# Query loads of the second half merged from four to two per pair, and the first two w_in tiles issued between the pairs

## The chip, the cores and the metric

One core of one Trainium2 chip. The metric is device time in microseconds (us) of one execution, taken as the median of several runs.

## What is computed

Attention with a bias that depends on the distance of two positions, followed by a two-layer MLP whose activation is the square of relu. Batch 4, 8 heads, 576 positions, head size 64; the MLP takes 2304 tokens of 512 to 2048 and back.

```python
scores = scale * np.matmul(q, k.transpose(0, 1, 3, 2))          # q, k, v: (4, 8, 576, 64)
x = (log1p(abs(i - j)) / log1p(max(i, 1)))[..., None]
bias = np.maximum(x @ w1 + b1, 0.0) @ w2                        # per head
attn = softmax(scores + bias, axis=-1)
y = np.matmul(attn, v)                                          # tokens of 512
out = np.maximum(y @ w_in, 0.0) ** 2 @ w_out                    # w_in (512, 2048), w_out (2048, 512)
```

## The kernel before

**Units and halves.** The heads are taken in pairs: `(b, hp)` is batch b and head pair hp. A unit `(b, hp, ic)` is one block of 128 query rows of one pair, both heads (ic 0 to 3), or the last 64 rows of both (ic 4, `TAIL`). There are 80 units (`units`, L125 to L127). The first 40 are batches 0 and 1 (`AB` = 2), ordered so that each block of bias is shared by all eight pairs. The second 40 (from `NA` = 40) are batches 2 and 3, ordered pair by pair: units 40 to 44 are the first pair, 45 to 49 the second.

**A unit.** `scores(u)` (L410) multiplies q and k on PE into the PSUM tile `sp` (one buffer), DVE adds the bias and finds the row maximum (L434, two instructions in a full unit; called the reduction below), ACT takes the exponential (L439). Two units later come `transposes` (PE L484, L487 and ACT copies L485, L488), then `values` (PE L502, and the DVE copy L507). After the last unit of a pair `normalise` and `scale_x` follow (PE L456, L470; DVE L473).

**Loads.** All loads are issued from the SP queue in one order. `load_k` makes two loads, `load_q` (L146) four: for each head one of 64 x 64 (the tail rows, L150) and one of 64 x 512 (L151) into a tile of 576 columns. In memory the queries lie as five blocks of 128 columns per head; in the last block the first head has its 64 rows in columns 0 to 63 and the second head in columns 64 to 127, and the rest is zero. In the second half k and q lie in tiles of which there are three, in space that the tiles of the first half leave.

**The loop** over s (L628) traces the program: at s = 40 it opens the pools of the second half and issues k and q of the first three pairs (L637 to L639); a further pair follows at s = 45, and so on; v loads come at L641.

**Weights.** w_in has 16 tiles of 512 KB. Before they can be used, their common scale must be known, so each is loaded once only for its largest element: `load_w` into a `stage` tile (two buffers) and `scan_w` (a DVE reduction, L189 reading `stage`). At s = 40 (`SC` - 1), after k and q of the three pairs, the first two are issued (L642 to L644). From s = 41 on, ten units hold the 16 scans, and each scan is followed by the load of the tile after next (L654) into the buffer that it frees. They are called w0 to w15 below, in the order of the scans. From s = 53 on the first 12 tiles are loaded again and split into two parts (`split_in`), between the units. The MLP follows.

**What sets the order.** A planner lays out the instructions of each queue (PE, DVE, ACT, POOL, SP) in advance from simulated times, and the hardware takes each queue in that order. `keep_in_program_order` pins an instruction behind what was traced before it on its engine: the scan of w0 thus can't be planned ahead of the reduction of unit 41, those of w1 and w2 not ahead of that of unit 42, and that of w3 not ahead of that of unit 43. What a scan waits for, everything behind it on DVE waits for too.

Of the kernel before, what the change touches and what calls it, by code (L numbers as in the profile page):

```python
# [10 lines left out]
F32 = mybir.dt.float32  # L11
# [10 lines left out]
B, H, S, D = 4, 8, 576, 64  # L22
# [5 lines left out]
AB = 2  # L28
NF = DFF // 128
NIC = 5  # L30
TAIL = 4
# [4 lines left out]
WB, WS, LW, XS, XB, LAG, NE, SC, SN, AH = 40, 3, 4, 48, 70, 1, 13, 22, 16, 2  # L36
# [13 lines left out]
SC = 41  # L50
# [29 lines left out]
def attention_then_relu2_mlp(ctx: ExitStack, tc: tile.TileContext, q, k, v, cols, w_in, w_out, psi, xmat, dist, out):  # L80
    nc = tc.nc
    PE, DVE, ACT, POOL, SP = nc.tensor, nc.vector, nc.scalar, nc.gpsimd, nc.sync
# [61 lines left out]
        v_t[b, hp] = t  # L144

    def load_q(b, hp):  # L146
        t = kq_p[-1].tile([128, S], F32, name="q1", tag="q1")
        for h in range(2):
            rows = slice(64 * h, 64 * h + 64)
            SP.dma_start(out=t[rows, 512:], in_=q[b, hp, TAIL, :, h, rows])  # L150
            SP.dma_start(out=t[rows, :512].rearrange("d (i m) -> d i m", i=TAIL), in_=q[b, hp, :TAIL, :, h].rearrange("i d m -> d i m"))  # L151
        q_t[b, hp] = t

    stage_p = {}
    w_t, wraw_t = {}, {}  # L160
# [249 lines left out]
    def scores(u):  # L410
        b, hp, ic = units[u]
        kt, qt = k1_t[b, hp], q_t[b, hp]
        negm = att.tile([128, 2], F32, name="negm", tag="negm", bufs=3)
        if (b, hp) not in sum_t:
            sum_t[b, hp] = att.tile([128, 9], F32, name="sums", tag="sums", bufs=AB * HP + 2)
        sums = sum_t[b, hp]
        p = att.tile([128, 2 * S], F32, name="p", tag="p", bufs=PB)

        nsp = 2 if ic < TAIL else 1
        sp4 = ps.tile([128, 4, 512], F32, name="sp", tag="sp", bufs=1)  # L420
        sps = [sp4[:, 2 * n:2 * n + 2] for n in range(nsp)]
        cols = slice(128 * ic, 128 * ic + 128 if ic < TAIL else S)

        for m, (x, h) in enumerate((x, h) for x in range(2) for h in (1, 0)):
            rows = slice(64 * h, 64 * h + 64)
            k0 = HALF * x + (64 if h and ic == TAIL else 0)
            out_t, to = (sps[h], slice(0, 128)) if ic < TAIL else (sps[0], rows)
            mm = PE.matmul(out_t[to, x, :HALF], lhsT=qt[rows, cols], rhs=kt[rows, k0:k0 + HALF], start=True, stop=True)  # L428
            if m:
                tc.keep_in_program_order(mm)  # L430
        for n, sp in enumerate(sps):
            bias = bias_t[:, 9 * hp + 2 * ic + n]
            t = att.tile([128, S], F32, name="t", tag="t", bufs=TB)
            DVE.tensor_tensor_reduce(  # L434
                out=t.rearrange("p (x n) -> p x n", x=2), in0=sp[:, :, :HALF],
                in1=bias.rearrange("p (x n) -> p x n", x=2), scale=-0.125, scalar=3.0e38,
                op0=ALU.add, op1=ALU.min, accum_out=negm[:, n:n + 1],
            )
            ACT.activation(out=p[:, S * n:S * n + S], in_=t, func=AF.Exp, bias=negm[:, n:n + 1], scale=-1.0, accum_out=sums[:, 2 * ic + n:2 * ic + n + 1])  # L439
        p_t[u] = p  # L440
        if ic == TAIL:
            POOL.tensor_copy(out=p[:, S:S + 64], in_=p[:, S - 64:S])
# [185 lines left out]
    for s in range(NU + TL + 1):  # L628
# [7 lines left out]
        for m, g in enumerate(groups[AB * HP:]):  # L636
            if s == max(first[g] - KL, NA):  # L637
                load_k(*g)
                load_q(*g)  # L639
            if s == max(first[g] - KL + TL + 1, NA - AB * HP + 2 + TL + m):  # L640
                load_v(*g)  # L641
        if s == SC - 1:  # L642
            load_w(ins[0])
            load_w(ins[1])  # L644
        for n in early:
            if when[n] == s + LW:
                load_w(n)
# [242 lines left out]
```

## Time and profile before

| | |
|---|---|
| median of 3 runs | 798.25 us (797.27 to 798.29) |
| profiled execution, its own time | 797.97 us |
| its span | 796.2 us |
| PE busy | 723.5 us, 91% of the span |
| DVE busy | 574.5 us, 72% |
| ACT busy | 456.5 us, 57% |
| DMA | 50.14 MB |

Times inside the execution are us from the start of the span. PE is TensorE's matmul, DVE VectorE, ACT ScalarE, POOL GpSimd; SPq is SP's queue, which issues loads. In a row of a timeline the number in square brackets is the time the engine was idle just before, with what ended it. The rows that matter stand in the section after the next.

### The profile page before, as it was taken

The numbers are of one execution on the slowest core, as the hardware profiler recorded it, in microseconds if no ns is written. First come the engines' busy times: TensorE is split into PE (matmuls) and PEld (weight loads), VectorE is DVE, ScalarE is ACT, GpSimd is POOL, SyncE is SP. The second block draws the span as 40 slices with busy tenths as digits, with TensorE's granted clock in tenths as the row PEclk, the third lists the DMA queues.
The fourth block names the chain that finished last, engine by engine and source line by source line (L and its number), as shares of the span: only waits on it lengthen the run. The fifth ranks groups of instructions, "written<-read, shape, count | busy, mean of one in ns | idle before, by whom it ended". The sixth has DMA issues, their size and how long they took to land.

```text
span 796.2 us, 17616 instructions
## 1 busy us (share of the span) xinstructions
PE 723.5 (91%) x7094; PEld 571.7 (72%) x7094; DVE 574.5 (72%) x1215; ACT 456.5 (57%) x940; POOL 186.4 (23%) x295
## 2 busy tenths in 40 slices
PE   5499999999988999979889899999989999999992
PEld 5456778787756676656677677878768887888881
DVE  7867778785666678898897979784845576557661
ACT  5757777777655678888676656664442233224220
POOL 1444333232210023342223324250400021000000
PEclk7869999999989999999999999999999999999997
DMA  7610000000376522301231143001010001000100
GB/s 203 191 60 18 3 16 2 3 2 2 105 239 232 189 85 85 111 28 54 80 107 54 67 146 107 28 22 59 26 54 1 1 1 54 1 1 1 54 2 27
DMA packets 27990, 50.14 MB, mean 63 GB/s; under 512 B 5252, under 2 KB 13444, under 8 KB 27908
## 3 DMA queue, kind: packets, MB, share of 16 engines
q1 hardware_dynamic: 27908, 49.01, 18.8%
q8 instruction: 56, 0.92, 0.5%
q14 instruction: 26, 0.21, 0.1%
HBM read 43.23 MB, written 5.77 MB: 62 GB/s over the span
## 4 chain that ended last, share of the span: by engine, by line
PE 50%; DVE 19%; ACT 8%; DMA 7%; SPq 6%; issue 5%; POOL 3%; DVEq 0%; ACTq 0%; POOLq 0%
PE y L766 16%; PE ha L717 8%; PE sp L428 7%; PE px L502 6%; PE hb L717 5%; PE pp L484 4%; PE bb L383 4%; DMA stage<-in_w_in 3%; DVE t L434 3%; ACT p L439 2%; SPq L150 2%; SPq L151 2%; DVE area L618 2%; DVE gl L747 1%; DVE wa L185 1%
## 5 line engine op out<-in xcount | busy, mean ns | idle before, releaser
L766 PE MATMUL y<-w,gh 128*128 128x512 f32 x576 | 177.9, 401 | 2.5 <-ACT gh L746 1.3
L717 PEld LDWEIGHTS <-area 128*128 128x128 f16 x1680 | 147.4, 99 | 42.5 <-issue 15.3
L439 ACT ACTIVATE p<-t,negm 128x576 f32<-128x576 f32 x144 | 111.2, 775 | 27.0 <-DVE negm L434 26.8
L434 DVE CUSTOM_DVE_ANT_0 t<-sp,area 128x576 f32<-128x576 f32 x144 | 104.1, 752 | 30.0 <-PE sp L428 21.3
L766 PEld LDWEIGHTS y<-w,gh 128*128 128x128 f32 x576 | 105.9, 190 | 24.9 <-ACT gh L746 2.9
L428 PE MATMUL sp<-k,q 64*128 64x288 f32 (+1 forms) x640 | 108.2, 447 | 15.0 <-DVE negm L434 11.4
L717 PE MATMUL ha<-area 128*128 128x256 f16 (+1 forms) x960 | 106.3, 266 | 9.0 <-DVE area L734 4.9
L766 PE MATMUL y<-w,gl 128*128 128x512 f32 x288 | 107.5, 397 | 1.1 <-DVE gl L747 1.1
L502 PE MATMUL px<-pt,v 128*64 128x128 f32 (+1 forms) x1600 | 96.6, 267 | 3.5 <-DVE xT L507 2.0
L485 ACT COPY pt<-pp 128x512 f32<-128x512 f32 x144 | 79.7, 582 | 32.0 <-PE pp L484 31.9
L502 PEld LDWEIGHTS px<-pt,v 128*64 128x64 f32 x1600 | 79.2, 137 | 19.7 <-issue 8.2
L484 PE MATMUL pp<-ident,p 128*128 128x128 f32 x576 | 84.5, 283 | 5.5 <-ACT pt L485 2.4
L428 PEld LDWEIGHTS sp<-k,q 64*128 64x128 f32 (+1 forms) x640 | 55.9, 182 | 41.1 <-DVE negm L434 15.3
L717 PE MATMUL hb<-area 128*128 128x256 f16 (+1 forms) x720 | 79.9, 262 | 1.4 <-DVE area L618 0.9
L484 PEld LDWEIGHTS pp<-ident,p 128*128 128x128 f32 x576 | 62.0, 142 | 22.8 <-issue 7.4
L398 POOL TENSOR_TENSOR area<-bt,bt 128x256 f32<-128x256 f32 x72 | 53.2, 763 | 81.9 <-DVE bt L393 81.9
L383 PE MATMUL bb<-wmov,mask 128*128 128x64 f16 x1440 | 52.6, 199 | 14.3 <-DVE bt L404 11.0
L766 PEld LDWEIGHTS y<-w,gl 128*128 128x128 f32 x288 | 53.8, 189 | 13.6 <-DVE gl L747 2.2
L383 PEld LDWEIGHTS <-mask 128*128 128x128 f16 x1440 | 48.2, 102 | 21.3 <-DVE bt L404 11.8
L369 DVE TENSOR_TENSOR mask<-sdist,theta 128x1024 f16<-128x1024 f16 (+1 forms) x78 | 49.7, 669 | 9.4 <-PE bb L383 9.4
L615 POOL TENSOR_TENSOR area<-xT 128x512 f32<-128x512 f32 (+1 forms) x17 | 22.8, 1344 | 143.2 <-DVE area L618 143.2
L747 DVE TENSOR_TENSOR gl<-area,gh 128x512 fp32r<-128x512 f32 (+1 forms) x40 | 30.2, 776 | 24.1 <-ACT gh L746 17.2
(153 smaller groups left out, 945.9 us busy)
## 6 DMA issues: line engine op xcount, KB each, us to landing
stage<-in_w_in SPq DMA_DIRECT2D x32, 512.0 KB, 4.2
stage<-in_w_out SPq DMA_DIRECT2D x16, 512.0 KB, 3.5
v<-in_v SPq DMA_DIRECT2D x16, 320.0 KB, 3.8
out<-o SPq DMA_DIRECT2D x18, 256.0 KB, 2.0
q<-in_q SPq DMA_DIRECT2D x32, 128.0 KB, 3.3
k<-in_k SPq DMA_DIRECT2D x16, 160.0 KB, 3.7
k<-in_k SPq DMA_DIRECT2D x16, 144.0 KB, 3.7
xc<-in_xmat SPq DMA_DIRECT2D x5, 288.0 KB, 3.6
```

The source lines that it names most:

```text
L369: DVE.tensor_tensor(out=m[:, :, :w], in0=win, in1=th.to_broadcast([128, 8, w]), op=ALU.is_ge)
L383: PE.matmul(bb[:, 64 * (7 - r):64 * (8 - r)], lhsT=m[:, r], rhs=wmov[:, n], start=(n == 0), stop=(n == 1))
L398: POOL.tensor_tensor(out=dst, in0=tw, in1=sw, op=ALU.add)
L428: mm = PE.matmul(out_t[to, x, :HALF], lhsT=qt[rows, cols], rhs=kt[rows, k0:k0 + HALF], start=True, stop=True)
L434: DVE.tensor_tensor_reduce(out=t.rearrange("p (x n) -> p x n", x=2), in0=sp[:, :, :HALF], in1=bias.rearrange("p (x n) -> p x n", x=2), sca ...
L439: ACT.activation(out=p[:, S * n:S * n + S], in_=t, func=AF.Exp, bias=negm[:, n:n + 1], scale=-1.0, accum_out=sums[:, 2 * ic + n:2 * ic + n ...
L484: PE.transpose(pp[:, 128 * c:128 * c + 128], p[:, k0:k0 + 128], ident)
L485: ACT.copy(pt[:, 4 * h:4 * h + 4], pp.rearrange("p (c m) -> p c m", c=4))
L502: PE.matmul(px[64 * h:64 * h + 64, :w], lhsT=vt[:, c, h], rhs=src, start=(c == 0), stop=(c == 4))
L717: PE.matmul(h[:, s, :w], lhsT=a, rhs=x, start=(k == 0), stop=(k == 5))
L747: DVE.tensor_tensor(out=gl, in0=g, in1=gh.bitcast(F32), op=ALU.subtract)
L766: PE.matmul(y, lhsT=a[:, slot, o:o + 128], rhs=x, start=((n, P) in firsts and f == 0 and m == 0), stop=((n, P) in lasts and f == 1 and m = ...
```

## The change

For batches 2 and 3 `load_q` makes one load per head: all five blocks of 128 columns go into a tile of 640 columns as they lie in memory, the zero columns too. The tail unit of the second head therefore reads its queries at column 576 instead of 512 (`q0`); all matmuls keep their shapes. And w0 is issued after k and q of the first pair and w1 after those of the second, instead of both after the third. The first half keeps its loads.

```diff
     def load_q(b, hp):
+        if b >= AB:
+            t = kq_p[-1].tile([128, NIC * 128], F32, name="q1", tag="q1")
+            for h in range(2):
+                SP.dma_start(out=t[64 * h:64 * h + 64].rearrange("d (i m) -> d i m", i=NIC), in_=q[b, hp, :, :, h].rearrange("i d m -> d i m"))
+            q_t[b, hp] = t
+            return
         t = kq_p[-1].tile([128, S], F32, name="q1", tag="q1")
...
-        cols = slice(128 * ic, 128 * ic + 128 if ic < TAIL else S)
...
+            q0 = 128 * ic + (64 if h and ic == TAIL and b >= AB else 0)
+            cols = slice(q0, q0 + (128 if ic < TAIL else 64))
...
                 load_k(*g)
                 load_q(*g)
+                if s == SC - 1 and m < 2:
+                    load_w(ins[m])
...
-        if s == SC - 1:
-            load_w(ins[0])
-            load_w(ins[1])
```

## Rows read from the trace of the kernel before

**Rows 1.** Timeline of DVE: start, duration, line, operation [idle before, releaser]

```profile
222.20 0.75 DVE L434 CUSTOM_DVE_ANT_0 t<-sp,area 128x576 f32<-128x576 f32 x1
...
223.93 0.22 DVE L473 TENSOR_TENSOR xT<-xT,rt 128x64 f32<-128x64 f32 x1
227.74 0.69 DVE L189 TENSOR_REDUCE small<-stage 128x1 f32<-128x512 f32 x1 [3.60 <-DMA stage<-in_w_in]
...
228.94 0.75 DVE L434 CUSTOM_DVE_ANT_0 t<-sp,area 128x576 f32<-128x576 f32 x1
...
230.29 0.68 DVE L189 TENSOR_REDUCE small<-stage 128x1 f32<-128x512 f32 x1
```

**Rows 2.** Timeline of PE, same columns

```profile
216.34 1.24 PE L428 MATMUL sp<-k,q 64*128 64x288 f32 x6
...
223.24 1.24 PE L428 MATMUL sp<-k,q 64*128 64x288 f32 x8
...
226.78 0.23 PE L456 MATMUL rp<-ident_b,parts 128*27 128x128 bf16 x1
230.43 2.29 PE L428 MATMUL sp<-k,q 64*128 64x288 f32 x8 [3.42 <-DVE negm L434]
```

**Rows 3.** Timeline of SP's queue: start, time to the group's end, line, load

```profile
210.02 0.47 SPq L137 DMA_DIRECT2D k<-in_k  x1
...
211.18 0.60 SPq L150 DMA_DIRECT2D q<-in_q  x1
...
213.56 0.62 SPq L151 DMA_DIRECT2D q<-in_q  x1
...
223.51 1.02 SPq L172 DMA_DIRECT2D stage<-in_w_in  x2
224.63 1.54 SPq L143 DMA_DIRECT2D v<-in_v  x3
228.46 2.87 SPq L172 DMA_DIRECT2D stage<-in_w_in  x2
```

**Rows 4.** Instructions of the tile stage, 200 to 300: ns min/median/max, first to last start

```profile
L189 DVE TENSOR_REDUCE small<-stage x16: 681/686/689, 227.7 to 270.0; 128x1 f32<-128x512 f32 x16
...
DMA to landing us min/median/max: 3.4/4.3/5.6
```

**Rows 5.** Stretches: busy of PE, PEld, DVE, ACT, POOL, PEclk, DMA share, GB/s

```profile
228.00:230.00 2.00, 0.00 (x0) 0.00 (x0) 2.00 (x5) 0.27 (x1) 0.00 (x0) 0.91 1.01 387
230.00:232.00 2.00, 1.57 (x6) 1.19 (x8) 1.17 (x4) 1.50 (x5) 0.00 (x0) 0.50 0.95 352
...
234.00:236.00 2.00, 2.00 (x9) 1.31 (x9) 1.88 (x6) 1.31 (x4) 0.00 (x0) 0.50 0.86 268
```

**Rows 6.** Chain that ended last, 223 to 270: start, us, what

```profile
231.00 5.57 DMA stage<-in_w_in
...
263.88 1.73 SPq L150
...
265.71 4.22 DMA stage<-in_w_in
```

**Rows 7.** Timeline of PE, later

```profile
250.84 1.31 PE L502 MATMUL px<-pt,v 128*64 128x128 f32 x20 [1.96 <-DVE xT L507]
...
271.57 0.35 PE L198 MATMUL pw<-small,ones 128*128 128x1 f32 x2 [0.72 <-DVE small L218]
```

**Rows 8.** Page, DMA issues: count, KB each, median us from issue to landing

```profile
k<-in_k SPq DMA_DIRECT2D x16, 160.0 KB, 3.7
...
q<-in_q SPq DMA_DIRECT2D x32, 16.0 KB, 2.9
```

**Rows 9.** Instructions of line 398, the last writers of the first half's bias

```profile
L398 POOL TENSOR_TENSOR area<-bt,bt x72: 721/737/1188, 46.6 to 181.1; 128x256 f32<-128x256 f32 x72
```

**Rows 10.** Stretches of the weight splits, columns as in Rows 5

```profile
300.00:350.00 50.00, 44.09 (x478) 31.94 (x472) 44.93 (x103) 42.18 (x97) 18.61 (x32) 1.00 0.24 78
350.00:400.00 50.00, 43.47 (x478) 32.78 (x474) 40.88 (x100) 37.60 (x84) 15.63 (x34) 0.97 0.21 72
```

## The prediction

> **What bounds the kernel now.** Over the whole span PE is the busiest engine, but an average says nothing about the one place that the change touches, so I read that place: the handover from the first half to the second, some 20 us after 210. I began with the DVE timeline, because the scans of w_in stand in it between the reductions that PE waits for. After the scaling of a finished pair had ended at 223.93 + 0.22 = 224.15, DVE sat idle for 3.60 us until w0 had landed at 227.74 [rows 1]. Behind that scan stands the reduction of unit 42, at 228.94. Its scores had been on PE at 223.24 for 1.24 us, so they were ready at 224.5: the reduction was some 4.4 us late, and only for the scan [rows 1, 2]. The scores of unit 43 need the PSUM buffer that this reduction empties. So PE ran dry at 226.78 + 0.23 = 227.0 and stood 3.42 us [rows 2]. That is one stall, seen on two engines; it counts once.
>
> Why w0 came late is in SP's queue. Its first load of the second half goes out at 210.02, and then k and q of three pairs, 6 loads each, fill the queue until w0 goes at 223.51. It lands 4.2 us later [rows 1, 3]. The 16 scans run from 227.7 to 270.0, one buffer being refilled while the other is scanned [rows 4]; the chain that ended last runs through such a refill at 231.00 (5.57 us) and one at 265.71 (4.22 us) [rows 6]. PE waits for this chain again at 250.84 (1.96 us, for a DVE copy queued behind a scan) and at 271.57 (0.72 us) [rows 7]. From 223 to 270, then, the time is set by scans and refills rather than by PE's work; what starts the scans earlier moves the whole stretch.
>
> **The change part by part.**
>
> *The queries.* A q load costs SP about the same whether small or large: the first is issued at 211.18, the fourth at 213.56, so (213.56 - 211.18) / 3 = 0.79 us apart, and one alone takes 0.60 or 0.62 [rows 3]. Two fewer save 1.2 to 1.6 us of SP per pair, 1.4 for the sum. The Trainium skill (DMA: Bandwidth & Descriptors, Rules for kernel authors) says that many small transfers should be made one, since under 64 KB one mostly pays overhead; the 16 KB load here took 2.9 us to land and the 160 KB one 3.7, so the trace bears that out, but it gives the sum nothing that SP's rows don't. A merged load of 160 KB should land like the k load of 160 KB, in 3.7 us [rows 8]. For the first pair the second q load goes out at about 212.0 and lands at 215.7; before, the fourth went at 213.56. PE reached the scores of unit 40 at 216.34 without having been idle [rows 2], so the earlier landing is worth nothing, and the 0.6 us between 215.7 and 216.34 is its cover. If the load lands like the slowest here, in 5.57 us [rows 6], PE waits 212.0 + 5.57 - 216.34 = 1.2 us. I take 0, ends 0 and a loss of 1.2. The 32 KB of zeros per head are in the same transfers and cost nothing of their own. The matmuls keep their shapes: nothing. The wider tile shifts where the three buffers lie in the space of the first half's tiles; these are all free when the last scores of that half are done, which is when the first k load went, so the loads can go no later for it: nothing.
>
> *w0 and w1.* In the new order w0 stands behind 4 loads instead of 18: 210.02 + two k loads at some 0.6 + two q loads at 0.6 to 0.8 gives 212.6 instead of 223.51, and w1 about 3.1 us later, at 215.7. Its wait: a stage buffer lies in space of the first half's preparation, whose last write ended soon after 181.1 [rows 9], long before. Even with the longest landing, 5.6 us [rows 4], w0 is there at 218.2 and w1 at 221.3. The scan of w0 can't be planned ahead of unit 41's second reduction, which follows that at 222.20 [rows 1]; so it finds its data, and starts when DVE comes to it, at 224.15: 227.74 - 224.15 = 3.6 us earlier. Unit 42's reduction follows at about 225.4, after its scores (224.5), so these don't hold it. The scan of w1 moves from 230.29 to 226.7 and finds its data too. w2 and w3 are issued when these two scans free the buffers, so they move by the same 3.6, and so on down the chain. k and q of the second and third pair now stand behind one or two weight tiles, 0.5 us of SP each, and share the DMA engines with them; they are needed five and ten units later, so this is hidden by some 15 us.
>
> *The refills beside the v loads.* Before, three v loads went out right behind w1 [rows 3], and at 228 to 230 the DMA engines were full (share 1.01, 387 GB/s) [rows 5]; w3's refill took 5.57 us against a median of 4.3 [rows 4, 6]. With SP empty some 4 us earlier these v loads mostly land before w2 and w3 are issued, so up to 5.57 - 4.3 = 1.3 us more. I take 0.7, ends 0 and 1.3.
>
> *The later q loads.* They stand on SP between refills. At 263.88 one took 1.73 us directly ahead of the refill that landed at 269.93 [rows 6], and behind that scan PE waited 0.72 us [rows 7]. With two q loads fewer that refill goes up to 2.3 us earlier, but PE can win only what it waited. I take 0.7, ends 0 and 1.5 (there are waits behind it too).
>
> *The clock.* After PE had been empty from 228 to 230 the granted clock was 0.50 from 230 to 236, the level of 1.2 GHz; PE was busy 1.57 + 2.00 + 2.00 = 5.6 us of it (three rows, the first and last shown) [rows 5]. At full clock that work would take 2.8 us less. But in that stretch PE runs beside the chain of scans, which waits for refills, so I take 0 for it; ends 0 and 2.8.
>
> *The rest.* Nothing after 270 is tied to a fixed time: the splits and the MLP start when what they read is there. I let the shift go through to the end.
>
> Sum: 3.6 + 0.7 + 0.7 = 5.0 us. Against the profiled execution, 797.97 us in all with a span of 796.2, that gives 793.0; the median of the runs is 0.28 above that execution, so the forecast of the median is **793.2**.
>
> **The rivals.**
>
> *The refill is held instead (A).* SP takes its loads in one order, and the w2 refill at 228.46 stands behind the v loads [rows 3]. A v load needs the buffer of a pair whose values are still being worked on; the last values of unit 39 end at about 226.8 on PE [rows 2]. If the planner puts that v load ahead of w2, w2 goes at 227.3 instead of 224.9. Then 228.46 - 227.3 = 1.2 us is left of the 3.6, and with half of the other terms (0.7) 798.25 - 1.9 = 796.4. The Trainium skill (DMA: Bandwidth & Descriptors, Anatomy of one DMA) says that a semaphore wait is taken by the issuing sequencer before a DMA goes out, which is how such a v load would hold what stands behind it; the order in the rows agrees. For this rival: three v loads follow right behind w1. Against it: SP had issued those three by 224.63 + 1.54 = 226.2, before the values of unit 39 ended.
>
> *Slower by the new plan (B).* All queues from unit 40 on are laid out anew. The tight place is the split of the first tiles, 300 to 400: DVE is busy 44.9 and 40.9 of 50 us, ACT 42.2 and 37.6, and PE stands 100 - 44.1 - 43.5 = 12.4 us [rows 10], since pieces of a split stand in DVE's and ACT's order ahead of a reduction or an exponential. If the new plan puts more of them ahead, PE's idle time grows. It decides from 5.0 + 1.6 = 6.6 us more, half as much again as now; at 8 us more the time is 798.25 + 3 = 801.3. For it: small gaps there depend on the order. Against it: the pieces and their pins are the same.
>
> *The clock counts in full (C).* If PE's slow work was on the path after all, 5.0 + 2.8 = 7.8 us: 790.4.
>
> *It doesn't do what it says (D).* If the planner leaves w0 behind the third pair, or its buffer comes free as late as that, only 2 x 3 loads' worth of SP is saved in front of it, 3 x 1.4 = 4.2 us. That would still cover the 3.6; only if SP is held elsewhere does 0.7 remain: 797.5.
>
> **How the numbers follow.** Forecast (790.8 to 795.5): 0.55. A: 0.20, B: 0.13, C: 0.08, D: 0.04. A measurement of this kernel can tell 0.2%, 1.6 us, so faster means under 796.65 and slower over 799.85. Faster is the forecast, C and 0.08 of A, whose price lies on the border: 0.71. Slower is B: 0.13. Between: 0.16. The range goes from 790.0, which leaves out half of C, to 798.6, which takes in A and D and leaves out B.
>
> **What would show it.** The first stage load on SP at about 212.6, with the k of the second pair behind it. The first scan on DVE at about 223 to 224 without a wait, and no stall of PE at 227; the granted clock at 1.00 from 228 to 238. The second and third refill (w2, w3) issued near 225 and 227.5, landing in about 4.3 us. The last scan near 265 instead of 270.0. If the first scan starts early and the last ends at 269 all the same, the chain is bound by its refills in a way I have not seen (A). If the last scan is 5 us early and the end is not, look at PE's idle time from 300 to 400 (B). A wait of PE for q at 216 would show that the w tiles slow the first pair's queries.

## The result, and the profile after

The changed kernel is slower: 801.42 us median (800.61 to 802.18, 4 runs) against 797.83 (797.27 to 798.29, 4 runs) of the kernel before, a ratio of 1.0057 with a 95% interval of 1.0038 to 1.0077. That is little, and it rests on four runs each; two more kernels with the same new order, run later beside the kernel before, were slower than it too (e2 and e3 below). The profiled execution took 802.18 us with a span of 800.4 (before: 797.97 and 796.2). Line numbers behind the new `load_q` are shifted: scores L430, reduction L436, exponential L441, scans L190, transposes L486 and L489, values L504, copies L509, weight loads L173; L150 is the merged q load.

The issues moved as forecast. This is SP's queue after, against [rows 3]:

```profile
209.53 1.69 SPq L150 DMA_DIRECT2D q<-in_q  x2
211.33 0.54 SPq L173 DMA_DIRECT2D stage<-in_w_in  x1
...
214.46 0.61 SPq L173 DMA_DIRECT2D stage<-in_w_in  x1
...
220.99 0.33 SPq L173 DMA_DIRECT2D stage<-in_w_in  x1
223.23 0.33 SPq L143 DMA_DIRECT2D v<-in_v  x1
```

w0 goes out 2.96 us after the first k load (208.37), where 13.5 us lay between them before. On DVE, against [rows 1], the scans of w0 and w1 find their data, and the stall has moved to w2:

```profile
220.28 0.68 DVE L190 TENSOR_REDUCE small<-stage 128x1 f32<-128x512 f32 x1
...
223.94 0.68 DVE L190 TENSOR_REDUCE small<-stage 128x1 f32<-128x512 f32 x1
227.80 0.69 DVE L190 TENSOR_REDUCE small<-stage 128x1 f32<-128x512 f32 x1 [3.18 <-DMA stage<-in_w_in]
228.40 0.28 DVE L509 COPY xT<-px 128x128 f32<-128x128 f32 x1
```

Two things are to be seen. The first scan starts 7.5 us earlier than before (220.28 against 227.74; 1.65 of it because this execution was that much ahead already at unit 39), more than was forecast. And the last line: a copy out of PSUM, of values that PE had started at 221.88 and finished 1.31 us later, at 223.2, stands behind three scans in DVE's order. PE pays for it, and also for a wait on q that wasn't there before; timeline of PE after, against [rows 2]:

```profile
213.72 1.33 PE L430 MATMUL sp<-k,q 64*128 64x288 f32 x8 [1.38 <-DMA q<-in_q]
...
225.34 0.66 PE L486 MATMUL pp<-ident,p 128*128 128x128 f32 x4
228.74 0.66 PE L486 MATMUL pp<-ident,p 128*128 128x128 f32 x4 [2.73 <-DVE xT L509]
```

The stretches after, columns as in [rows 5], show PE empty at 226 to 228 and the clock at the 1.2 GHz level behind it, and the DMA engines nearly full from 212 on:

```profile
212.00:214.00 2.00, 0.62 (x12) 0.52 (x14) 1.80 (x6) 0.33 (x3) 0.98 (x5) 1.00 0.92 264
...
220.00:222.00 2.00, 1.71 (x13) 0.95 (x13) 2.00 (x6) 2.00 (x6) 0.36 (x1) 1.00 1.15 224
...
226.00:228.00 2.00, 0.00 (x1) 0.00 (x0) 0.20 (x1) 0.58 (x1) 0.00 (x0) 1.00 0.84 329
...
230.00:232.00 2.00, 2.00 (x21) 1.56 (x17) 0.12 (x2) 1.70 (x6) 0.00 (x0) 0.50 0.52 209
```

The tile stage after, against [rows 4], and the chain that ended last, against [rows 6]. The scans start 7.5 us earlier and the last starts where it did before (269.9 against 270.0), and two refills of that chain took 6.78 and 7.35 us, where the longest landing before was 5.6 [rows 4]:

```profile
L190 DVE TENSOR_REDUCE small<-stage x16: 674/686/700, 220.3 to 269.9; 128x1 f32<-128x512 f32 x16
...
DMA to landing us min/median/max: 3.3/4.7/7.5
```

```profile
220.99 6.78 DMA stage<-in_w_in
...
240.07 7.35 DMA stage<-in_w_in
...
264.92 4.99 DMA stage<-in_w_in
```

At the end of this stretch PE waits three times and then runs slow. Timeline of PE after, against [rows 7], and two stretches of it:

```profile
266.67 1.24 PE L430 MATMUL sp<-k,q 64*128 64x288 f32 x8 [1.41 <-DVE negm L436]
269.05 1.31 PE L504 MATMUL px<-pt,v 128*64 128x128 f32 x20 [1.15 <-DVE xT L509]
272.57 1.24 PE L430 MATMUL sp<-k,q 64*128 64x288 f32 x8 [2.20 <-DVE small L218]
...
275.07 2.40 PE L504 MATMUL px<-pt,v 128*64 128x128 f32 x20
```

```profile
270.00:272.00 2.00, 0.37 (x8) 0.12 (x4) 1.93 (x6) 0.22 (x1) 0.00 (x0) 1.00 0.89 295
...
274.00:276.00 2.00, 2.00 (x17) 1.67 (x18) 1.84 (x8) 0.98 (x3) 0.00 (x0) 0.54 0.02 8
```

The values at 275.07 took 2.40 us for what takes 1.31 at full clock. Before, the row sum `pw` and the transposes stood ahead of the scores of unit 52 there, and PE waited 0.72 us [rows 7]. After, they stand behind them, and PE waits 2.20.

To see where the time went I took, for each unit, the end of its last reduction on DVE, counted from that of unit 39, and subtracted the same of the kernel before. Negative is ahead of the kernel before. The column heads are the experiments below.

| unit (before, us) | after | e1 | e2 | e4 | e6 | e10 | e11 | e12 |
|---|---|---|---|---|---|---|---|---|
| 42 (230.3) | -4.70 | -3.73 | +0.27 | -3.99 | -3.73 | -3.73 | -3.73 | -3.73 |
| 43 (235.1) | +0.77 | -4.00 | +3.80 | -0.04 | -3.73 | -4.96 | -2.25 | -3.56 |
| 45 (244.9) | +1.27 | -4.51 | +3.82 | +0.47 | -4.24 | -6.18 | -2.91 | -2.65 |
| 47 (255.4) | +0.55 | -4.02 | +2.05 | -1.15 | +0.21 | -3.88 | +1.52 | -3.61 |
| 50 (266.9) | +1.17 | -4.17 | +1.13 | -1.21 | -0.47 | -4.04 | +1.11 | -2.85 |
| 52 (275.7) | +1.25 | -3.09 | +3.13 | -0.42 | +0.85 | -3.25 | +3.69 | -1.70 |
| 53 (279.3) | +4.54 | -3.09 | +5.98 | -0.42 | +4.66 | -3.26 | +4.89 | +0.75 |
| 54 (281.6) | +4.55 | -3.09 | +5.99 | -0.42 | +4.68 | -3.25 | +4.89 | +0.77 |
| 78 (383.7) | +4.55 | -2.79 | +6.07 | -0.37 | +4.72 | -3.04 | +4.31 | +1.04 |

After unit 53 the lag of the changed kernel stays as it is up to unit 78: the splits of 300 to 400 [rows 10] and all of attention behind them add nothing. The 5 us or so were lost between 210 and 280. The MLP behind it added 1.3 us to the lag in this one execution; in those of the columns e1, e6 and e10 it took 2.4, 2.0 and 3.9 us off, so what a single execution does there says little.

### The profile page after: what moved, and what is told of

It reads as the page before. It is cut to its first block, busy times and chain, and to the rows that moved or that the text cites. A ratio compares the mean times of both kernels' runs of the same rounds, so it can differ in the third digit from the quotient of the medians.

```text
span 800.4 us, 17593 instructions
## 1 busy us (share of the span) xinstructions
PE 720.8 (90%) x7094; PEld 569.8 (71%) x7094; DVE 576.9 (72%) x1215; ACT 455.7 (57%) x940; POOL 188.5 (24%) x295
## 4 chain that ended last, share of the span: by engine, by line
PE 52%; DVE 22%; ACT 8%; DMA 7%; issue 5%; POOL 3%; SPq 0%; DVEq 0%; ACTq 0%; POOLq 0%
PE y L767 16%; PE sp L430 7%; PE ha L718 7%; PE px L504 6%; PE hb L718 5%; PE pp L486 5%; PE bb L384 4%; DMA stage<-in_w_in 3%; DVE t L436 3%; DVE gl L748 2%; ACT p L441 2%; DVE area L620 2%; DMA stage<-in_w_out 1%; DVE wa L186 1%; DVE area L229 1%
## 5 line engine op out<-in xcount | busy, mean ns | idle before, releaser
L441 ACT ACTIVATE p<-t,negm 128x576 f32<-128x576 f32 x144 | 111.2, 776 | 26.2 <-DVE negm L436 26.1
L436 DVE CUSTOM_DVE_ANT_0 t<-sp,area 128x576 f32<-128x576 f32 x144 | 103.9, 751 | 29.6 <-PE sp L430 26.2
L430 PE MATMUL sp<-k,q 64*128 64x288 f32 (+1 forms) x640 | 106.2, 440 | 17.2 <-DVE negm L436 10.7
L504 PE MATMUL px<-pt,v 128*64 128x128 f32 (+1 forms) x1600 | 98.7, 271 | 4.3 <-DVE xT L509 2.6
L504 PEld LDWEIGHTS px<-pt,v 128*64 128x64 f32 x1600 | 80.9, 139 | 20.9 <-issue 7.2
L486 PE MATMUL pp<-ident,p 128*128 128x128 f32 x576 | 84.0, 282 | 7.4 <-DVE xT L509 2.7
L430 PEld LDWEIGHTS sp<-k,q 64*128 64x128 f32 (+1 forms) x640 | 55.4, 179 | 41.9 <-issue 13.9
L486 PEld LDWEIGHTS pp<-ident,p 128*128 128x128 f32 x576 | 61.8, 142 | 25.0 <-issue 7.2
L384 PE MATMUL bb<-wmov,mask 128*128 128x64 f16 x1440 | 50.9, 196 | 14.3 <-DVE bt L405 11.0
L748 DVE TENSOR_TENSOR gl<-area,gh 128x512 fp32r<-128x512 f32 (+1 forms) x40 | 32.4, 831 | 24.5 <-ACT gh L747 17.7
```

What stands on the lines that cost most here:

```text
L384: PE.matmul(bb[:, 64 * (7 - r):64 * (8 - r)], lhsT=m[:, r], rhs=wmov[:, n], start=(n == 0), stop=(n == 1))
L436: DVE.tensor_tensor_reduce(out=t.rearrange("p (x n) -> p x n", x=2), in0=sp[:, :, :HALF], in1=bias.rearrange("p (x n) -> p x n", x=2), sca ...
L486: PE.transpose(pp[:, 128 * c:128 * c + 128], p[:, k0:k0 + 128], ident)
L504: PE.matmul(px[64 * h:64 * h + 64, :w], lhsT=vt[:, c, h], rhs=src, start=(c == 0), stop=(c == 4))
L748: DVE.tensor_tensor(out=gl, in0=g, in1=gh.bitcast(F32), op=ALU.subtract)
```

## The experiments

Two explanations stood against each other from here. **Theory O**: the planner laid out PE's, DVE's and ACT's queues anew, and it is this new order that costs. The instructions are the same; from unit 40 on they stand in another order, and before that in the same one. **Theory L**: the loads collide. SP now issues w0, w1 and the merged q loads so closely that the DMA engines are nearly full from 212 on (share 0.92 to 1.15), refills land late, and everything behind a scan is held.

To part order from loads I made kernels that carry the planned order of another kernel along: each instruction of PE, DVE and ACT between two marks is tied to the one ahead of it in a recorded list. No semaphore wait is added by that; only the planner is bound, and POOL's queue, which the expectation of e1 names too, is left to it. "Old order" is the order of the kernel before, "new order" that of the changed kernel. All ratios are to runs of the kernel before, made beside each kernel; single executions of one kernel with ten or more runs spread over 4 to 9 us there, and so a lag in the table, which is that of one execution, counts only where the ratio agrees.

| | loads | order | median us (runs) | ratio | 95% interval |
|---|---|---|---|---|---|
| after | new | new | 801.42 (4) | 1.0057 | 1.0038 to 1.0077 |
| e1 | new | old | 795.23 (12) | 0.9982 | 0.9966 to 0.9998 |
| e2 | old | new | 804.60 (4) | 1.0099 | 1.0082 to 1.0116 |
| e3 | q merged alone | its own, the new one | 803.59 (6) | 1.0092 | 1.0072 to 1.0112 |
| e4 | w0, w1 moved alone | its own, nearly the old one | 798.22 (12) | 1.0015 | 0.9991 to 1.0039 |
| e5 | new | new to unit 46, then old | 794.57 (10) | 0.9986 | 0.9965 to 1.0006 |
| e6 | new | old to unit 46, then new | 801.85 (4) | 1.0073 | 1.0046 to 1.0099 |
| e7 | new, q rows contiguous | old | 795.38 (12) | 0.9984 | 0.9963 to 1.0006 |
| e8 | new | its own, scans tied behind copies | 799.31 (12) | 1.0043 | 1.0022 to 1.0065 |
| e9 | new | new, old at unit 52 | 800.78 (12) | 1.0043 | 1.0020 to 1.0065 |
| e10 | q of a pair in one load | old | 793.99 (12) | 0.9965 | 0.9940 to 0.9990 |
| e11 | new | old, new for units 47 to 50 | 798.63 (12) | 1.0014 | 0.9987 to 1.0041 |
| e12 | new | old, new from unit 52 on | 798.85 (12) | 1.0033 | 1.0008 to 1.0057 |

### e1: the new loads in the old order

```diff
+def queues_as_recorded(tc):
...
+    traced = {}
+    for i in tc.nc.cur_bb.bb.instructions:
+        traced.setdefault(str(i.engine), []).append(i)
+    dep = mybir.DependencyInfo(mybir.DependencyClass.NoSync, mybir.DependencyReason.DATA)
+    for e, order in json.loads(zlib.decompress(base64.b85decode(RECORDED))).items():
+        for x, y in zip(order, order[1:]):
+            tc.add_manual_dep(traced[e][y], traced[e][x].name, dep, reason="recorded order")
...
         attention_then_relu2_mlp(tc, **args)
+        queues_as_recorded(tc)
```

`RECORDED`, left out here, holds the order of the kernel before.

> The loads of the changed kernel, but PE, DVE, ACT and POOL take their instructions in the order of the kernel before. Theory L (early w tiles and merged q loads fill the DMA engines from 212 to 226, so that the refill of w2 and the first q land late, and that is the loss): still slow, 800 to 802 us. Theory O (the planner's new order costs the time, the loads themselves gain): 793 to 796 us. Both half: 797 to 799.

Measured: 0.9982, faster than the kernel before by 1.4 us (0.2 to 2.7), and 6 us faster than the changed kernel, whose loads are the same. DVE's timeline of this kernel:

```profile
223.86 0.68 DVE L190 TENSOR_REDUCE small<-stage 128x1 f32<-128x512 f32 x1
...
226.40 0.68 DVE L190 TENSOR_REDUCE small<-stage 128x1 f32<-128x512 f32 x1
227.00 0.28 DVE L509 COPY xT<-px 128x128 f32<-128x128 f32 x1
228.94 0.69 DVE L190 TENSOR_REDUCE small<-stage 128x1 f32<-128x512 f32 x1 [1.67 <-DMA stage<-in_w_in]
```

w0 and w1 are scanned without a wait at 223.86 and 226.40 (the forecast said 224.15 and 226.7), and the copy stands ahead of the scan of w2, not behind it. Unit 42 is 3.73 us ahead. The DMA engines are just as full as in the changed kernel, 1.02 over 212 to 226 at 272 GB/s against 1.05 at 274, and here it costs a wait of 1.67 us on DVE. Theory L alone can't be the loss.

### e2: the old loads in the new order

The same edit on the kernel before, with the order of the changed kernel recorded.

> The loads of the kernel before (four q loads, w0 and w1 behind the third pair), but the compute queues in the order of the changed kernel. Theory O: the order alone costs the loss and w0 comes late as well, 801 to 805 us. Theory L: the order costs nothing, 797 to 799 us.

Measured: 1.0099, that is 7.9 us slower (6.5 to 9.2) with not one load changed. Timeline of PE of this kernel:

```profile
216.10 1.31 PE L428 MATMUL sp<-k,q 64*128 64x288 f32 x8 [2.31 <-DMA q<-in_q]
...
228.02 0.41 PE L470 MATMUL ra<-rows,pick 27*64 27x128 bf16 x8 [2.32 <-DVE xT L473]
...
230.58 2.29 PE L428 MATMUL sp<-k,q 64*128 64x288 f32 x8 [2.10 <-DVE negm L434]
```

The new order asks for q earlier, and PE stands 2.31 us for it, with transposes and values of earlier units behind the scores that it could have done; the second and third row show two more waits, for DVE. With e1 this is a square of four kernels: the loads are worth -1.4 us in the old order and 4.5 - 7.9 = -3.4 in the new one (each within 1.3 and 2.1), and the order costs +7.9 with the old loads and some +6 with the new. Order is the loss, and the loads are a gain in both, a small one in the old.

### e3 and e4: which half of the change brings the new order

e3 has the merged q loads alone (the diff without its last two parts), e4 the moved weight loads alone (only those).

```diff
                 load_k(*g)
                 load_q(*g)
+                if s == SC - 1 and m < 2:
+                    load_w(ins[m])
...
-        if s == SC - 1:
-            load_w(ins[0])
-            load_w(ins[1])
```

This is e4, with the q loads of before.

> Only the q loads are merged; w0 and w1 stay behind the third pair. The planner lays out the same compute order as for the whole change. Theory O: slow like the old loads in the new order, 800 to 804 us. Theory L: the w tiles are no longer in the way of q, so about 797 to 799 us.

> Only w0 and w1 are moved between the pairs; q comes in four loads. The planner keeps the order of the kernel before but for a few DVE instructions. Theory O: the stall at the first scan goes and nothing else changes, 793 to 796 us. Theory L: the w tiles fill the DMA engines ahead of the v loads and w2, so 798 to 802 us.

e3 gave 1.0092, and its planned order of PE, DVE and ACT is that of the changed kernel, instruction for instruction. So merging the q loads is what turns the order over. PE's order in the traces is the same in both, too. e4 keeps the old order but for a few DVE instructions, and gains nothing that can be told from zero: 1.0015; its 798.22 us lie at the lower end of what theory L gave. What took the gain is seen in SP's queue and in DVE's timeline of this kernel:

```profile
218.47 0.60 SPq L172 DMA_DIRECT2D stage<-in_w_in  x1
...
225.08 1.50 SPq L143 DMA_DIRECT2D v<-in_v  x3
226.67 0.86 SPq L172 DMA_DIRECT2D stage<-in_w_in  x2
```

```profile
222.65 0.68 DVE L189 TENSOR_REDUCE small<-stage 128x1 f32<-128x512 f32 x1
...
226.11 0.69 DVE L189 TENSOR_REDUCE small<-stage 128x1 f32<-128x512 f32 x1
232.68 0.69 DVE L189 TENSOR_REDUCE small<-stage 128x1 f32<-128x512 f32 x1 [5.88 <-DMA stage<-in_w_in]
```

The buffer of w2 was free when the scan of w0 ended at 222.65 + 0.68 = 223.33, but the refill went out only at 226.67, behind the last q loads of the third pair and three v loads. It landed some 6.0 us later, where w2 in e1 took 4.4; that part speaks for theory L. The lag jumps from -3.99 to -0.04 at unit 43. So the two halves need each other: without the merge SP holds the refill, and without the move there is only the new order. In the ratios e4 and e1, which differ in the merge alone, lie 2.6 us apart, little more than their intervals (some 2.3).

### e5 and e6: which part of the new order

Both have the new loads. The two orders hold the same instructions up to a cut between units 46 and 47, so one can follow the other there. The edit is that of e1 with another list in `RECORDED`: for e5 that of the changed kernel up to the cut and that of the kernel before behind it, for e6 the other way round.

> The changed kernel's loads; the compute queues follow its own new order up to unit 46 and the order of the kernel before from there on. If the two losses seen from unit 39 on (the gain of 4 us gone by unit 46, 3 us more at unit 53) have separate causes, the first stays and the second goes: about 0 against the kernel before at unit 46 and within 1 us of that at the end, 797 to 799 us. If the early order is the cause of both, 801 to 803 us.

> The reverse: the order of the kernel before up to unit 46, the new order after it. Separate causes: 4 us ahead at unit 46, then 3 to 4 us lost at units 50 to 53, 797 to 799 us. If the late loss only follows from the early one: 4 us ahead to the end, 793 to 796 us.

e5 0.9986, e6 1.0073: outside what the expectations allowed. Both looked for a loss in the early part of the order (e5 at 797 to 799 or 801 to 803 us, measured 794.57; e6 at 797 to 799 or 793 to 796, measured 801.85). The new order of units 40 to 46, with its wait for q, costs nothing that these runs can tell (0.3 us against e1, within some 2); that from 47 on costs. The profiled execution of e5, the slowest of its ten, shows that it can cost in a single one: 1.57 us ahead at unit 43 where e1 was 4.00, and 0.36 behind at unit 54. PE waited for q there, and the granted clock was at 0.50 from 216 to 218 behind it:

```profile
215.32 2.38 PE L430 MATMUL sp<-k,q 64*128 64x288 f32 x8 [1.59 <-DMA q<-in_q]
```

The order from 47 on, put into e1, makes e6, (1.0073 - 0.9982) x 797 = 7.3 us; put into e5 it makes the changed kernel, 5.7 us (each within some 2.5, the root of the sum of the squares of both half-intervals). What the two orders are around there, on PE, first the new and then the old:

```
unit 47  new: pa 44 | px 43 | sp 47          old: sp 47 | pa 44 | px 43
unit 48  new: px 44 | rp | sp 48             old: sp 48 | px 44 | rp
unit 52  new: sp 52 | pw | pp 49 | pa 49     old: pw | pp 49 | pa 49 | sp 52
```

Timeline of PE in e6 at those places, and two stretches of it:

```profile
247.50 1.80 PE L504 MATMUL px<-pt,v 128*64 128x128 f32 x20 [3.34 <-DVE xT L509]
...
252.25 1.24 PE L430 MATMUL sp<-k,q 64*128 64x288 f32 x8
...
272.14 2.29 PE L430 MATMUL sp<-k,q 64*128 64x288 f32 x8 [2.17 <-DVE small L218]
```

```profile
248.00:250.00 2.00, 2.00 (x20) 1.67 (x17) 1.01 (x4) 1.01 (x4) 0.00 (x0) 0.54 0.24 82
...
272.00:274.00 2.00, 1.86 (x8) 1.27 (x8) 0.32 (x3) 0.98 (x4) 0.00 (x0) 0.52 0.46 176
```

and the same place in e1:

```profile
246.67 1.31 PE L504 MATMUL px<-pt,v 128*64 128x128 f32 x20 [2.30 <-DVE xT L509]
247.91 0.66 PE L486 MATMUL pp<-ident,p 128*128 128x128 f32 x4
248.50 1.24 PE L430 MATMUL sp<-k,q 64*128 64x288 f32 x8
...
268.32 0.35 PE L199 MATMUL pw<-small,ones 128*128 128x1 f32 x2 [0.95 <-DVE small L219]
...
269.72 1.24 PE L430 MATMUL sp<-k,q 64*128 64x288 f32 x8 [0.45 <-DVE negm L436]
```

In e1 PE waits too, 2.30 us, for a copy behind the scan of a late refill; but the scores of unit 47 come 1.83 us after that wait ends, and the clock stays at 1.00 from 246 to 250. In e6 they come 4.75 us after it, behind all values and transposes, at a clock of 0.54 to 0.60 from 248 to 252, so the reduction, the exponential and everything that hangs on unit 47 start later: the lag goes from -2.70 at unit 46 to +0.21 at 47. At unit 52 the scores wait for the reduction of unit 51, which stands behind the last scan, and in the new order nothing is left ahead of them: PE was 0.00 busy from 270 to 272 and then ran at half clock.

### e11 and e12: the late part cut once more

e11 has the old order with the new one for units 47 to 50 alone, e12 with the new one from unit 52 on alone.

> The changed loads in the order of the kernel before, but units 47 to 50 stand as the changed kernel plans them: on PE the scores behind the tail transposes and values (or the row factors) of earlier units, on DVE the copies out of PSUM ahead of the reductions. With the new order from unit 46 to the end the time was 801.85, with the old order throughout 795.2, so 7.3 us (1.0073 against 0.9982) lie between units 46 and the end. Theory O1 (each place costs by itself): the lags in that run's profile put 4 to 5 us at units 46 to 50 and 3.8 at 53; then this kernel takes 795.2 + 4.5 = 799.7, ratio 1.002 to 1.005, lag at unit 54 about +0.5 to +1.5. Theory O2 (the places cost only together, through PE running empty twice and the clock): under 2 us, ratio below 1.0005, lag at unit 54 below -1.5.

> The changed loads in the order of the kernel before up to unit 51, and from unit 52 on as the changed kernel plans them: the scores of unit 52 ahead of the small chain's row sum and the tail's transposes on PE, its reduction ahead of the chain on DVE, and the small differences in the MLP. Theory O1: 3.3 to 3.8 us at unit 53 and 1.3 more in the MLP; 795.2 + 4.5 = 799.7 at most, ratio 1.001 to 1.004, lag stepping from -3 at unit 52 to about +0.5 at 53. Theory O2, and what the run with the old order at unit 52 alone showed (0.6 us gained in the median): little is tied to this place; lag after unit 53 about -2.5, ratio below 1.000.

e11 1.0014, e12 1.0033: against e1 that is (1.0014 - 0.9982) x 797 = 2.6 us and 4.1 us (each within some 2.5). Together 6.7, and e6, whose order differs from that of e1 by just these two parts, lost 7.3. e12 lies where O1 put it: the part from unit 52 on costs by itself, and that the places cost only together (O2) doesn't fit it. e11 lies between the bands of O1 (from 1.002) and O2 (under 1.0005); that units 47 to 50 cost by themselves is only just outside the noise. The part from unit 52 on also takes in small differences in the MLP, which these runs don't part from unit 52. The profiled execution of e11 was the slowest of its twelve (801.56 against a median of 798.63), which fits that its lags are larger than its ratio. In e12 the lag steps by 2.45 us between units 52 and 53, where the stretches are these:

```profile
268.00:270.00 2.00, 0.00 (x0) 0.00 (x0) 1.93 (x6) 0.51 (x1) 0.00 (x0) 1.00 0.74 248
270.00:272.00 2.00, 1.72 (x8) 1.19 (x8) 0.47 (x5) 1.12 (x4) 0.00 (x0) 0.62 0.55 213
272.00:274.00 2.00, 2.00 (x10) 1.36 (x8) 1.43 (x5) 0.02 (x1) 0.00 (x0) 0.53 0.01 2
```

PE is empty for two microseconds and then at the 1.2 GHz level for some three. It stood 2.33 us before the scores where e1 stood 0.95 + 0.45 before `pw` and the scores, 0.9 more; and the scores took 2.14 us instead of 1.24, `pw` 0.58 instead of 0.35, four transposes 1.09 instead of 0.63, the tail 0.38 instead of 0.27, together 1.7 more. In this execution the slow clock behind the wait cost more than the additional wait.

### e9: the changed kernel with unit 52 alone put back

The edit is again that of e1 with another list: that of the changed kernel, but with 10 instructions of PE and 11 of DVE at unit 52 in the order of the kernel before.

> The changed kernel in its own planned order, but for one place: at unit 52 the row sum of the small chain (pw), the transposes and the tail's transposes stand ahead of the scores of unit 52 on PE, and the small chain ahead of the reduction of that unit on DVE, as the kernel before has them (10 PE and 11 DVE instructions trade places). Theory O, late part: in the changed kernel PE waits 2.20 us for the small chain before the scores of unit 52 and then runs at the 1.2 GHz level; the lag against before steps from +1.3 at unit 52 to +4.5 at 53. With the old order there, the step is gone: lag at unit 54 about +1.3 (0 to +2), granted clock 1.00 at 274 to 278, time 801.4 - 3.2 = 798.2 (797 to 799.5), ratio 0.999 to 1.002. Rival: the step is the wait for the last refill (w15 is scanned at 269.9 in both kernels), and the order at unit 52 only shows it; then the lag at unit 54 stays at +3.5 to +4.5 and the time at 801.

Measured 1.0043, outside the range that theory O gave (0.999 to 1.002): 1.1 us better than the changed kernel where 3.2 was expected, and within the two intervals (some 2.4) not to be told from nothing nor from 3.2. The time is what the rival said (801), the lag at unit 54 in the one trace, +1.6, what theory O said, so e9 decides nothing between them; e12 speaks for theory O. In the trace of e9 PE runs slow from 268 to 275 all the same, since it had stood 1.61 and 1.29 us behind scans that waited 2.06 and 1.05 us for their refills. So PE waited there in the old order as well.

### e8: the scans kept behind the copies

```diff
     def scan_w(k):
-        tc.keep_in_program_order(largest(wraw_t.pop(ins[k])[:, :, :, 1].bitcast(F32), wcols[:, k:k + 1]))
+        scan = tc.keep_in_program_order(largest(wraw_t.pop(ins[k])[:, :, :, 1].bitcast(F32), wcols[:, k:k + 1]))
+        tc.add_manual_dep(scan.ins, evac[-1].name, mybir.DependencyInfo(mybir.DependencyClass.NoSync, mybir.DependencyReason.DATA), reason="evacuate first")
...
-            DVE.tensor_copy(out=xT[b][:, hp, end - w:end], in_=px[:, :w])
+            evac.append(DVE.tensor_copy(out=xT[b][:, hp, end - w:end], in_=px[:, :w]).ins)
```

> The whole change with the planner free, but each scan is tied behind the last DVE copy out of PSUM (values) traced before it, so that no such copy waits behind a scan for a refill. If these copies are what makes the new order slow: 794 to 798 us. If something else in the new order is: 800 to 803 us.

Measured 1.0043 against 1.0057: not told apart, and at 799.31 us between the two expectations. The planner is free here and only each scan is pinned behind the last copy traced before it. It does what the pin says: no stall of PE at 228, and units 42, 46 and 47 are 5.1, 3.9 and 3.7 us ahead. But PE then waits 4.02 us for the small chain, ahead of the scores of unit 52:

```profile
269.02 2.29 PE L432 MATMUL sp<-k,q 64*128 64x288 f32 x8 [4.02 <-DVE small L220]
```

The lag goes from -1.0 at unit 52 to +2.0 at units 53 and 54. A pin on this one kind of instruction did not mend the order as a whole.

### e7 and e10: larger pieces, fewer loads

In e7 the queries lie so that a row of 640 columns is one piece of 2560 B instead of five of 512 B; in e10 one load of 320 KB brings both heads of a pair. Both are in the old order, and both lay q out anew before it reaches the chip, so the loads of the first half read the same bytes from other places.

```diff
             for h in range(2):
-                SP.dma_start(out=t[64 * h:64 * h + 64].rearrange("d (i m) -> d i m", i=NIC), in_=q[b, hp, :, :, h].rearrange("i d m -> d i m"))
+                SP.dma_start(out=t[64 * h:64 * h + 64], in_=q[b, hp, h])
...
```

That is e7; e10 has one line in place of the loop:

```diff
-            for h in range(2):
-                SP.dma_start(out=t[64 * h:64 * h + 64].rearrange("d (i m) -> d i m", i=NIC), in_=q[b, hp, :, :, h].rearrange("i d m -> d i m"))
+            SP.dma_start(out=t, in_=q[b, hp].rearrange("h d m -> (h d) m"))
...
```

> New loads in the old order, and q laid out in memory so that a partition's 640 columns are one piece of 2560 bytes instead of five of 512. Theory L (what is left of it: the small pieces keep the DMA engines full from 212 to 226 and delay w2): the waits for w2 (1.7 us) and a late refill (2.4 us) shrink and the time is 1 to 3 us under that of the new loads in the old order. If the pieces don't matter: the same as that, within 1 us.

> The changed loads in the order of the kernel before, but q lies so that both heads of a pair come in one load of 320 KB for all 128 partitions, 2560 B in a row of each. One SP instruction fewer per pair than with two loads. Theory O: the loads' gain is set by the start of the scans, which find w0 and w1 in place already; the fewer issues take 0.7 us off the queue per pair and give at most the late refill waits, so lag about -3.7 at unit 54 and to the end, time 795 (793.5 to 796), ratio 0.996 to 0.9995. Theory L: the engines are what is short at 212 to 226, and fewer, larger pieces bring w2 earlier; then the lag at unit 43 is -4.5 or more and the time 794 or less.

e7 0.9984, the same as e1, with a DMA share of 0.97 against 1.02 from 212 to 226: a larger piece gained nothing. e10 0.9965, 2.8 us faster than the kernel before (0.8 to 4.8) and the fastest of all kernels here; its interval overlaps that of e1. Timeline of DVE of e10, and the stretches of e10 and then of e1:

```profile
227.96 0.69 DVE L189 TENSOR_REDUCE small<-stage 128x1 f32<-128x512 f32 x1 [0.71 <-DMA stage<-in_w_in]
```

```profile
226.00:240.00 14.00, 13.24 (x143) 9.09 (x139) 10.41 (x26) 8.04 (x22) 0.24 (x1) 1.00 0.86 279
```

```profile
226.00:240.00 14.00, 12.67 (x131) 9.04 (x128) 10.52 (x25) 7.00 (x20) 0.24 (x1) 0.88 0.84 261
```

w2 lands 1 us earlier (a wait of 0.71 where e1 had 1.67), the clock stays at 1.00 from 226 to 240 (0.88 in e1), and unit 43 is 4.96 us ahead. The expectation had named -4.5 at unit 43 as the mark of theory L; so theory L holds for about a microsecond of the w2 refill. The lead grows to 6.18 us at unit 45, but only 3.88 is left at unit 47 and 3.25 at unit 54, about as in e1: PE was busy 0.63 and 0.81 us of the two stretches of 2 us from 242 to 246, and from 246 to 248 the clock was at 0.50. The time, 793.99, lies where the two forecasts meet. The Trainium skill (DMA: Bandwidth & Descriptors, Rules for kernel authors) advises one transfer over 128 partitions instead of two over its halves. The ratios go that way, 0.9965 for one load and 0.9984 for two (e7), but their intervals overlap, so no run here shows it.

## Why the prediction was wrong

**What bounds the kernel: right.** The wait for w0, and with it the place of w0 in SP's queue, was worth what was said, as far as unit 42. In e1 the scan of w0 starts at 223.86 without a wait, and unit 42 is 3.73 us ahead where the prediction had 3.6.

**The queries: right on SP, wrong on PE.** Two merged loads take SP 1.29 to 1.71 us, where 1.2 to 1.6 was taken, and w0 went out at 212.82 in e1 and w1 at 215.97 (forecast 212.6 and 215.7). "PE reached the scores of unit 40 at 216.34 without having been idle, so the earlier landing is worth nothing" holds in e1, where PE takes them at 216.14 after no wait. In the changed kernel they stand right behind `rt`, ahead of transposes and values that take 2.3 us in e1 (213.83 to 216.14), and PE waits 1.38 us. The cover of 0.6 us was a property of the old order: with the old loads in the new order PE waits 2.31 us for q (e2), so the early w tiles, which the prediction named for such a wait, are not needed for it. The zeros in a merged load are 160 - 144 = 16 KB per head, not 32; 32 is the figure for a pair.

**The failed step** is the one that wasn't written down as a step: every part of the sum read each engine's order off the trace of before (the scan of w0 after 224.15, the scores of unit 40 at 216.34, the row sum ahead of unit 52) and let only the times move. The prediction says that all queues from unit 40 on are laid out anew, but in rival B only, and only for the stretch of 300 to 400. Merging the q loads was enough to turn the planner's choices (e3). That term should have stood in the sum at some +6 (e1 to after) or +7.9 (e2), larger than all the others together. The planner works from simulated times, and the loads come into those; why it chose as it did is argued from this, not shown.

**The refills beside the v loads (0.7): the size fits in the old order.** The lead of e1 grows from 3.73 at unit 42 to 4.58 at 44, 0.85 more, though DVE waited 1.67 us for w2; that the refills made it isn't shown. In the changed kernel w2's refill took 6.78 us and DVE waited 3.18: w2 was asked for at 220.99, right behind the loads of the third pair and two v loads, since the new order scans w0 some 2 us earlier still, counted from unit 39.

**The later q loads (0.7): not won.** In e1 no q load stands ahead of the last refill any more, which goes at 260.50 instead of 265.71, but it took 6.19 us where 4.22 was read before. The lead falls from 4.17 at unit 50 to 3.09 at 51, where the scan of w14 waits 2.44 us for its refill. The last scan starts at 266.71, not near 265.

**The clock (0): right for the sum, but the price came from the other side.** It wasn't won where it was looked for (0.50 to 0.70 from 230 to 234 after); it was lost at 274 to 278 after, where PE had not been slow before, and in e6 and e12 behind the empty stretches shown above.

**To the end: right up to unit 78.** What is ahead or behind at unit 54 is still so at unit 78, within 0.6 us in every column; for the MLP behind it the runs don't show it. The 5.0 us of the sum, which is a forecast for the loads alone, stand against 3.1 at unit 54 and 1.4 (0.2 to 2.7) in the medians of e1, and 2.8 (0.8 to 4.8) in e10. So the loads too were worth less than the sum. The first two terms, 4.3, were there at unit 44 (4.58); the third was not won, and 1.5 of the lead went by unit 54. Why the medians of e1 show less than its trace isn't settled; that trace is of an execution of 792.82 us, 2.4 faster than the median.

**The rivals.** The sign that the prediction gave for A came: the first scan early, the last at 269.9 all the same. Its cause did not: w2's refill went at 220.99, when the scan of w0 ended at 220.28 + 0.68 = 220.96, so nothing held it on SP. A held refill is seen in e4, where without the merge w2 waits 3.3 us on SP and the lead goes. B had the right kind of cause, in the wrong place: 300 to 400 runs in parallel with before. That its time is nearly right (801.3 against 801.42) is luck: it sets 8 us against a gain of 5.0, where the runs show 6 to 7.9 against 1.4 to 3.4. Its chance of 0.13 was argued from that stretch alone, where the pieces and their pins are the same; the stretch where the change acts was not weighed. C and D are out: w0 went at 211.33, and the clock cost time.

**Open.** How the 6 us divide between units 47 to 50 and the part from unit 52 on isn't settled: put into the old order the two cost 2.6 and 4.1 us, but putting unit 52 right in the changed kernel gave back 1.1, and all these differ by little more than their intervals. And theory L's share in the changed kernel, where refills took 6.8 and 7.4 us, wasn't parted from the order that asked for them at that moment.

## What to carry to other kernels

Where a planner lays out the queues, a changed load is also a changed order: first compare the two planned orders engine by engine, and cost the new places (what now stands ahead of what, and which wait it will meet) before costing the load. To find out which of the two made a difference, run each kernel's loads in the other's order; four kernels part them. In a stretch that waits for refills, the instruction that can fill a wait is worth more ahead of the one that must wait: in e6 and e12 the empty PE paid twice, once by waiting and once by the clock behind it.

## What the runs showed of the hardware

- The DMA engines were full at quite different rates: share 1.15 at 224 GB/s (220 to 222 after) and 1.01 at 387 and 389 GB/s (228 to 230 before, 224 to 226 after), where by SP's queue it was mostly w tiles and v that were in flight. Rows of 2560 B instead of 512 B for q changed neither the time (e7 against e1) nor the rate much: e10, also with long rows, had 0.97 at 275 GB/s over 212 to 226, e1 1.02 at 272. What holds the rate down with q and k in flight stays open.
- The same load landed at quite different times: the 160 KB k load of the second half took 3.0 us before and 5.4 in the changed kernel (medians of 200 to 230), where SP issued its loads more closely and the DMA share from 212 to 222 was 0.92 to 1.15 instead of 0.45 to 0.64. A 512 KB tile took between 3.3 and 7.5 us in the changed kernel.
- After PE had been empty for two microseconds (e6 270 to 272, e12 268 to 270, after 226 to 228), the granted clock was at 0.50 to 0.62, the 1.2 GHz level for most of it, in the two-microsecond stretch next to it or the one after that, with PE busy 1.72 to 2.00 us of the stretch, and back at 1.00 by 274 (e12) and 234 (after).
- It doesn't follow each time, nor for a given wait: in e2 PE was empty from 214 to 216 (a wait of 2.31 us) and the clock stayed at 1.00 in the stretches behind it, while in e5 a wait of 1.59 us at the same scores left it at 0.50 from 216 to 218. What decides it isn't shown.
